# Score blocks with v and k with v in 64x64 tiles of TensorE, by token halves in two turns

## The chip, the cores and the metric

The kernel runs on one core of one Trainium2 chip. The metric is the device time of one execution in microseconds (us); before the change it is the median of three runs.

## The reference

Attention first: for each batch b (4) and head h (8) a state of 48 x 48 is carried over 768 tokens. Then a feed-forward layer with a leaky activation over all 3072 tokens.

```python
B, H, S, D = 4, 8, 768, 48
for t in range(S):
    kt, vt, rt = k[:, :, t], v[:, :, t], r[:, :, t]
    cur = einsum('bhd,bhe->bhde', u[None] * kt, vt)
    y[:, :, t] = einsum('bhd,bhde->bhe', rt, state + cur)
    state = w[None, :, :, None] * state + einsum('bhd,bhe->bhde', kt, vt)
x = y.transpose(0, 2, 1, 3).reshape(B * S, H * D)   # 3072 x 384
h = x @ w_in                                         # 384 x 2048
g = maximum(h, 0) + alpha * minimum(h, 0)
out = g @ w_out                                      # 2048 x 384
```

## The kernel before

The tokens are cut into six chunks of 128 (C = 6, L = 128). In each chunk the eight heads are worked in four pairs (q = 0 to 3); the two heads of a pair (g = 0, 1) lie on partitions 0 to 47 and 64 to 111. For a pair `attention` makes:

- the raw loads of r, k and v, and on VectorE r and k scaled by powers of w (L397);
- on TensorE the scores A = k^T r (from chunk 2 on in `triangle`, L441; in chunks 0 and 1 L450), each batch a block of 128 key tokens x 128 query tokens;
- `base`, which is the diagonal term u on the diagonal (ScalarE, L465, from the table `ident`) and the scores strictly above it (VectorE predicated copies with the mask `strict4`, L473);
- on TensorE the output y in `out`: from the state T with r (L514), then from v with `base` (L519), and, but for the last chunk, the state product of k with v (`state_product`, L528);
- y split into a high and a low half in SBUF, `x` (ScalarE L567, VectorE L571), and the state's update T (VectorE L626).

From chunk 2 on the scores are a triangle: with the key tokens in two halves of 64, the second half of the keys meets only the second half of the queries. `triangle` makes the first half's columns 128 wide and the second half's 64 wide, in 64x64 tiles, and leaves the other block out. For odd batches the key halves are swapped on the partitions, so that four tiles (row half by head, column half by key half) work side by side. The output from v and `base` still uses all 128 partitions of key tokens and all 128 query columns, in tiles of 128 rows and 64 columns; the parts of `base` in the left-out block are zeros.

The results of y go to two PSUM banks, `y[0]` (name "y", one buffer) and `y[1]` (name "hp", two buffers, which the feed-forward layer's input products use as well). Bank g holds the part of head g of the state term. The state product lies behind y in the bank "y".

From chunk 2 on `pair` puts the scores of pair q and the output and state product of pair q - 1 into one piece of work on TensorE. The first pair of a chunk has its scores alone, and the output of the last pair is a piece of its own.

The feed-forward layer runs beside it: `m_in` and `m_in_two` (L803, L756) make hp = w_in x for 128 of the 2048 columns, or for two such pieces at once with seven products in place of eight; VectorE and ScalarE make g and its halves gh and gl (L787 to L814); `m_out` (L845) adds w_out g to three banks `acc`. These are in fp32r and three products each (high with high, low with high, high with low).

The order of all instructions is written out by a planner (`Plan`): each piece has an engine, an estimated time, its reads and writes, and a rank; twelve rounds of list scheduling, forward and backward, choose the order with the earliest end. A bank that one engine reads is not read by another at the same time, so pieces of VectorE and ScalarE on one bank follow each other. Where the change gives pieces other times or other buffers, the planner makes a new order for the whole kernel.

Of the kernel before, what the change touches and what calls it, by code (L numbers as in the profile page):

```python
# [195 lines left out]
def rwkv_prelu_kernel(ctx: ExitStack, tc, rk, vkr, wP, uP, u, wall, alpha, w, r_all, k_all, v_all, oT):  # L196
# [30 lines left out]
    strict4 = fixed([128, B, L], "strict4", U8)  # L227
# [40 lines left out]
    def swapped_masks():  # L268
        add("POOL", 0.3, lambda: nc.gpsimd.memset(ones(), 1.0), w=[ones], rank=10)
        for rows, base in ((slice(0, HI), -HI), (slice(HI, 128), 0)):  # L270
            add("POOL", 0.3, lambda rows=rows, base=base: nc.gpsimd.affine_select(
                ones()[rows], ones()[rows], pattern=[[1, 128]], base=base, channel_multiplier=-1,
                compare_op=ALU.is_gt, fill=0.0), w=[ones], rank=10)
        for b in range(B):
            add("POOL", 0.3, lambda b=b: nc.gpsimd.tensor_copy(strict4()[:, b], (ones if b % 2 else strict)()),
                r=[ones, strict], w=[(strict4, b)], rank=10)
        for h in range(2):
            add("ACT", 0.5, lambda h=h: nc.scalar.activation(
                wtok()[HI * h:HI * h + HI, :, 1], wtok()[HI - HI * h:128 - HI * h, :, 0], AF.Copy), r=[(wtok, 0)],
                w=[(wtok, 1 + h)], rank=10)  # L280
# [82 lines left out]
    def attention(c, q, at):  # L363
# [3 lines left out]
        def swap(b):  # L367
            return c > 1 and b % 2 == 1

# [64 lines left out]
        A = [pb([128, B, L], f"A{g}" if not first or q % 2 == 0 else f"acc{g}") for g in range(2)]  # L434

        def triangle():

            for rows, j in ((0, 0), (0, 1), (1, 0), (1, 1)):
                for b, g in ((2 * j, 0), (2 * j + 1, 0), (2 * j, 1), (2 * j + 1, 1)):
                    o, t = (rows + b) % 2, slice(HI * rows, L)  # L440
                    nc.tensor.matmul(A[g]()[HI * o:HI * o + HI, b, t], k0()[half(g), b, HI * rows:HI * rows + HI],  # L441
                                     r()[half(g), b, t], start=(rows == 0 and j == 0), stop=(rows == 1 and j == 1),
                                     skip_group_check=True)
# [13 lines left out]
        base = [sb([128, B, L], "base", 4) for _ in range(2)]  # L457
        for g in range(2):
# [5 lines left out]
            for b in range(B):  # L464
                add("ACT", 0.39, lambda g=g, b=b: nc.scalar.activation(  # L465
                    base[g]()[:, b].rearrange("p (a t) -> p a t", a=2),
                    ident().rearrange("p (a t) -> p a t", a=2)[:, ::-1 if swap(b) else 1], AF.Copy,
                    scale=cu()[:, g, (b if c < 2 else place[b]):][:, 0:1]), r=[cu, ident], w=[(base[g], b)],
                    rank=at - 0.9 if c != 1 else -50)
        parts = [(slice(0, 128), slice(0, B), slice(HI, L)), (slice(0, HI), slice(0, B, 2), slice(0, HI)),  # L470
                 (slice(HI, 128), slice(1, B, 2), slice(0, HI))]
        for g, at_part in [(g, x) for g in range(2) for x in parts] if c > 1 else ():
            add("DVE", 0.42 if at_part is parts[0] else 0.28, lambda g=g, x=at_part: nc.vector.copy_predicated(  # L473
                base[g]()[x], strict4()[x], A[g]()[x]), r=[strict4, A[g]], w=[base[g]], rank=at - 1.5)
# [9 lines left out]
        U, plain = None, c < 2  # L484
# [4 lines left out]
        else:  # L489
            y = [pb([112, 2 * 2 * L], "y"), pb([112, 2 * L], "hp", 2)]  # L490
            U, mine = y[0], (y[0], "U")
            y_of = [(y[0], "y"), y[1]]

        def u_rows(rows):
            return U()[rows].rearrange("p (b e) -> p b e", b=B) if plain else \
                U()[rows, 2 * L:2 * L + B * D].rearrange("p (b e) -> p b e", b=B)

        def out():
            if plain:
                for b in range(B):  # L500
                    for g in range(2):
                        rows, x = (slice(0, HI) if g == 0 else half(g)), g * B + place[b]
                        nc.tensor.matmul(y()[rows, b], v().rearrange("p x e -> p (x e)")[  # L503
                            :, x * D:x * D + rows.stop - rows.start], base[g]()[:, b], start=b == 0,
                            stop=first and b == B - 1, skip_group_check=True)
                for b in () if first else range(B):
                    for g in range(2):
                        nc.tensor.matmul(y()[half(g), b], T[q]()[half(g), b], r()[half(g), b], start=False,  # L508
                                         stop=(b == B - 1), skip_group_check=True)
                return  # L510
            for j in range(2):
                for g, o in ((0, 0), (1, 1), (0, 1), (1, 0)):
                    b = j + 2 * (g ^ o)
                    nc.tensor.matmul(y[g]()[half(o), j * L:(j + 1) * L], T[q]()[half(g), b], r()[half(g), b],  # L514
                                     start=(j == 0), stop=False, skip_group_check=True)
            for j in range(2):
                for g, o in ((0, 0), (1, 1), (1, 0), (0, 1)):
                    b = j + 2 * (g ^ o)
                    nc.tensor.matmul(y[g]()[half(o), j * L:(j + 1) * L], v()[:, g * B + place[b]], base[g]()[:, b],  # L519
                                     start=False, stop=(j == 1), skip_group_check=True)  # L520
# [602 lines left out]
```

## Time and profile before

| | |
|---|---|
| device time, median of three runs | 501.57 us (501.52 to 501.6) |
| span of the profiled execution, first to last instruction | 499.7 us |
| what lies around the span (501.57 - 499.7) | 1.9 us |
| TensorE busy | 491.7 us, 98% of the span |
| VectorE, ScalarE, GpSimd busy | 373.7, 267.1, 51.4 us |
| granted clock of TensorE, mean | 0.997 of full speed |

No time of its own is listed for the profiled execution beside its span; its own time is taken as the span and the 1.9 us around it, which is the median of the runs. In the rows, PE is TensorE's matmuls, PEld its weight loads, DVE VectorE, ACT ScalarE, POOL GpSimd; L519 is line 519 of the kernel before; "y<-base,v" names the output and the inputs. A matmul of float32 operands leaves two records in the trace. Matmuls overlap, so the distance between starts says more than their durations.

### The profile page before, as it was taken

What the parts mean: (1) busy time and instruction counts of PE and PEld (TensorE: products, weight loads), DVE (VectorE), ACT (ScalarE), POOL (GpSimd) and SP (SyncE); (2) the same over time, 40 slices, a digit from 0 to 9 for tenths busy, and PEclk for the clock granted to TensorE, in tenths of its full rate; (3) what the DMA queues carried; (4) which work ended last, traced back from release to release, by engine and by line L of the source; (5) the groups of instructions that cost most, each with busy time, mean ns of one, the idle gap of its engine ahead of it and who ended that gap; (6) DMA issues with size and microseconds to landing.
All of it is one profiled execution on the core that took longest, in us unless ns stands there. A gap on an engine that the chain in (4) does not pass through costs nothing.

```text
span 499.7 us, 9759 instructions
## 1 busy us (share of the span) xinstructions
PE 491.7 (98%) x3817; PEld 405.8 (81%) x3817; DVE 373.7 (75%) x677; ACT 267.1 (53%) x612; POOL 51.4 (10%) x56
## 2 busy tenths in 40 slices
PE   8999999999999999999999999999999999999995
PEld 6877777888788887888888888888788888898984
DVE  6799999899985997768699476789475676445451
ACT  3898786786652555535455555355554443533322
POOL 4200140001020130011030020232000000000000
PEclk9999999999999999999999999999999999999998
DMA  8796765530132633313130322140230000100001
GB/s 235 240 291 193 233 202 182 190 143 1 61 124 79 184 113 96 133 35 83 56 102 30 102 68 62 54 136 16 82 72 1 0 1 1 63 1 1 2 1 68
DMA packets 24020, 46.72 MB, mean 94 GB/s; under 512 B 3488, under 2 KB 11680, under 8 KB 23968
## 3 DMA queue, kind: packets, MB, share of 16 engines
q1 hardware_dynamic: 23712, 46.03, 29.9%
q8 instruction: 32, 0.52, 0.4%
q14 instruction: 20, 0.16, 0.1%
q10 hardware_dynamic: 256, 0.00, 0.0%
HBM read 37.37 MB, written 6.29 MB: 87 GB/s over the span
## 4 chain that ended last, share of the span: by engine, by line
PE 93%; ACT 3%; DVE 1%; DMA 1%; issue 0%; ACTq 0%; DVEq 0%
PE acc L845 38%; PE hp L803 19%; PE hp L756 19%; PE A L441 3%; PE y L519 2%; PE hp L519 1%; PE y L514 1%; PE A L450 1%; PE y L503 1%; ACT base L465 1%; PE y L528 1%; PE A L845 1%; PE y L508 1%; PE acc L854 1%; PE hp L925 1%; DMA wp<-wP 1%
## 5 line engine op out<-in xcount | busy, mean ns | idle before, releaser
L803 PE MATMUL hp<-x,wh 128*128 128x512 f32 x288 | 98.1, 398 | 0.1
L845 PE MATMUL acc<-gh,wh 128*128 128x512 f32 (+1 forms) x282 | 79.9, 391 | 0.0
L845 PE MATMUL acc<-gh,wl 128*128 128x512 f32 (+1 forms) x282 | 79.6, 390 | 0.0
L845 PE MATMUL acc<-gl,wh 128*128 128x512 f32 (+1 forms) x282 | 79.5, 390 | 0.0
L787 DVE TENSOR_TENSOR g<-hp,g 128x512 f32<-128x512 f32 x48 | 32.7, 689 | 53.4 <-PE hp L756 45.0
L803 PEld LDWEIGHTS hp<-x,wh 128*128 128x128 f32 x288 | 54.0, 188 | 14.0 <-DVE g L810 0.8
L792 ACT ACTIVATE gh<-g 128x512 fp32r<-128x512 f32 x48 | 30.2, 632 | 61.2 <-DVE g L789 53.1
L756 PE MATMUL hp<-x,wh 128*128 128x256 f32 (+1 forms) x192 | 62.1, 346 | 0.0
L845 PEld LDWEIGHTS acc<-gh,wl 128*128 128x128 f32 x282 | 51.5, 188 | 11.1 <-issue 0.2
L845 PEld LDWEIGHTS acc<-gl,wh 128*128 128x128 f32 x282 | 51.2, 188 | 10.6
L465 ACT ACTIVATE base<-ident,cu 128x128 f32<-128x128 f32 x176 | 57.3, 390 | 4.3 <-DVE cu L430 3.1
L768 ACT ACTIVATE g<-hp 128x256 f32<-128x256 f32 x96 | 34.3, 381 | 46.2 <-PE hp L756 44.7
L845 PEld LDWEIGHTS acc<-gh,wh 128*128 128x128 f32 x282 | 50.7, 188 | 10.0
L803 PE MATMUL hp<-x,wl 128*128 128x512 f32 x144 | 56.8, 395 | 0.0
L810 DVE SCALAR_TENSOR_TENSOR g<-hp,alph,g 128x512 f32<-128x512 f32 x48 | 35.9, 748 | 23.0 <-ACT g L809 22.7
L424 POOL TENSOR_TENSOR rr<-rr,kk 128x384 f32<-128x384 f32 x16 | 19.4, 1212 | 275.3 <-DMA kk<-vkr 120.5
L809 ACT ACTIVATE g<-hp 128x512 f32<-128x512 f32 x48 | 28.5, 594 | 33.9 <-PE hp L803 32.8
L814 DVE TENSOR_TENSOR gl<-g,gh 128x512 fp32r<-128x512 f32 x48 | 33.7, 701 | 12.9 <-ACT gh L813 7.9
L813 ACT ACTIVATE gh<-g 128x512 fp32r<-128x512 f32 x48 | 30.2, 629 | 23.0 <-DVE g L810 21.6
L756 PEld LDWEIGHTS hp<-x,wh 128*128 128x128 f32 x192 | 36.1, 188 | 5.9 <-ACT g L768 1.4
L793 DVE TENSOR_TENSOR gl<-g,gh 128x512 fp32r<-128x512 f32 x48 | 34.6, 729 | 4.1 <-ACT gh L792 1.0
L397 DVE TENSOR_TENSOR raw<-raw,W 112x512 f32<-112x512 f32 x45 | 36.0, 810 | 0.3
(186 smaller groups left out, 851.2 us busy)
## 6 DMA issues: line engine op xcount, KB each, us to landing
wraw<-wall SPq DMA_DIRECT2D x16, 768.0 KB, 5.0
raw<-rk SPq DMA_DIRECT2D x45, 224.0 KB, 3.1
v<-vkr SPq DMA_DIRECT2D x24, 192.0 KB, 3.5
kk<-vkr SPq DMA_DIRECT2D x21, 192.0 KB, 3.1
rr<-vkr SPq DMA_DIRECT2D x16, 192.0 KB, 2.5
oT<-o SPq DMA_DIRECT2D x12, 256.0 KB, 2.3
x<-x SPq DMA_DIRECT2D x36, 64.0 KB, 2.8
oT<-g SPq DMA_DIRECT2D x5, 256.0 KB, 2.1
```

What stands on the lines that cost most here:

```text
L397: add("DVE", 0.72 if c < 2 else 0.85, lambda t=t, tab=tab: nc.vector.tensor_tensor(out=t(), in0=t(), in1=tab().broadcast_to([112, B, L]), ...
L465: add("ACT", 0.39, lambda g=g, b=b: nc.scalar.activation(base[g]()[:, b].rearrange("p (a t) -> p a t", a=2), ident().rearrange("p (a t) -> ...
L756: nc.tensor.matmul(bank()[:, cols], ws[a], xs[b], start=start and j == 0, stop=stop and j == 2, skip_group_check=True)
L768: add("ACT", 0.37, lambda: nc.scalar.activation(t()[:, cols], bank()[:, src], AF.Copy), r=[bank], w=[(t, part)], rank=rank - 100).early = 0.3
L787: add("DVE", 0.75, lambda g=g, bank=bank: nc.vector.tensor_tensor(out=g(), in0=bank(), in1=g(), op=ALU.add), r=[bank], w=[g], rank=m - 100)
L792: add("ACT", 0.64, lambda g=g, gh=gh: nc.scalar.activation(gh(), g(), AF.Copy), r=[g], w=[gh], rank=m - 100)
L793: add("DVE", 0.73, lambda g=g, gh=gh, gl=gl: nc.vector.tensor_tensor(out=gl(), in0=g(), in1=gh(), op=ALU.subtract), r=[g, gh], w=[gl], ran ...
L803: nc.tensor.matmul(hp(), a[i]()[:, k], x[c]()[:, k], start=(k == 0 and j == 0), stop=(k == NK - 1 and j == 2))
L810: add("DVE", 0.75, lambda: nc.vector.scalar_tensor_tensor(out=g(), in0=hp(), scalar=alph()[:, i:i + 1], in1=g(), op0=ALU.mult, op1=ALU.max ...
L813: add("ACT", 0.64, lambda: nc.scalar.activation(gh(), g(), AF.Copy), r=[g], w=[gh], rank=n - 100)
L814: add("DVE", 0.73, lambda: nc.vector.tensor_tensor(out=gl(), in0=g(), in1=gh(), op=ALU.subtract), r=[g, gh], w=[gl], rank=n - 99)
L845: nc.tensor.matmul(bank(), a[i]()[:, NK + k], x()[:, cols], start=(begin and j == 0), stop=(end and j == 2), skip_group_check=(c == C - 1))
```

## The change

From chunk 2 on:

- The scores' bank is laid out in blocks of 64 columns: slots 0 to 3 hold the diagonal blocks of the four batches (both key halves, one on each partition half), slots 4 and 5 the full blocks of first-half keys with second-half queries. `base` has the same layout. The diagonal term is then written into 64-column blocks from a table `eye`; per head one predicated copy takes slots 0 to 3 and one plain copy slots 4 and 5.
- The output from v and `base` is made by key halves (`out_of_tokens`), each with 64 rows and 64 columns of the array: the first key half of a batch with 128 columns, the second with 64. The zero block is left out.
- The state product is made by token halves too (`state_of_tokens`).
- Two row halves of the array write two different banks. So each of both products is done in two turns: in turn 0 row half n writes bank n, in turn 1 the other one. Turn 1 begins with an instruction on TensorE that does nothing but wait for the last matmul of turn 0 (`in_turn`).
- The joint piece of TensorE is now: state part and turn 0 of pair q - 1, scores of pair q, turn 1 of pair q - 1. For the last pair of a chunk, turn 1 follows turn 0 directly, and its state product lies in the scores' banks A0 and A1.
- The state product of the other pairs lies behind y in both banks, "y" and "hp", and the state's update is two VectorE instructions, one a bank.
- The masks on GpSimd are made for halves, and the planner gets other times for the pieces.

The core of the diff:

```diff
-        A = [pb([128, B, L], f"A{g}" if not first or q % 2 == 0 else f"acc{g}") for g in range(2)]
+        tri = c > 1
+        A = [pb([128, 8, HI] if tri else [128, B, L], f"A{g}" if not first or q % 2 == 0 else f"acc{g}")
+             for g in range(2)]
+
+        def blocks(b):
+
+            return slice(b, None, 4 + b // 2 - b)
...
                     o, t = (rows + b) % 2, slice(HI * rows, L)
-                    nc.tensor.matmul(A[g]()[HI * o:HI * o + HI, b, t], k0()[half(g), b, HI * rows:HI * rows + HI],
-                                     r()[half(g), b, t], start=(rows == 0 and j == 0), stop=(rows == 1 and j == 1),
-                                     skip_group_check=True)
+                    to = A[g]()[HI * o:HI * o + HI]
+                    nc.tensor.matmul(to[:, b] if rows else to[:, blocks(b)][:, 0:2],
+                                     k0()[half(g), b, HI * rows:HI * rows + HI],
+                                     r()[half(g), b, t], start=(rows == 0 and j == 0),
+                                     stop=(rows == 1 and j == 1), skip_group_check=True)
...
-        for g, at_part in [(g, x) for g in range(2) for x in parts] if c > 1 else ():
-            add("DVE", 0.42 if at_part is parts[0] else 0.28, lambda g=g, x=at_part: nc.vector.copy_predicated(
-                base[g]()[x], strict4()[x], A[g]()[x]), r=[strict4, A[g]], w=[base[g]], rank=at - 1.5)
+        for g in range(2) if tri else ():
+            add("DVE", 0.42, lambda g=g: nc.vector.copy_predicated(base[g]()[:, 0:B], strict4(), A[g]()[:, 0:B]),
+                r=[strict4, A[g]], w=[(base[g], b) for b in range(B)], rank=at - 1.5)
+            add("DVE", 0.28, lambda g=g: nc.vector.tensor_copy(base[g]()[:, B:B + 2], A[g]()[:, B:B + 2]),
+                r=[A[g]], w=[(base[g], B)], rank=at - 1.5)
...
-            y = [pb([112, 2 * 2 * L], "y"), pb([112, 2 * L], "hp", 2)]
-            U, mine = y[0], (y[0], "U")
-            y_of = [(y[0], "y"), y[1]]
+            y = [pb([112, 4 * L], "y"), pb([112, 4 * L], "hp", 2)]
+            U, u0, mine = y, 2 * L, [(t, "U") for t in y]
+            if alone:
+                U = mine = [pb([112, NT], f"A{g}") for g in range(2)]
+                u0 = 0
+            y_of = [(t, "y") for t in y]
...
-            for j in range(2):
-                for g, o in ((0, 0), (1, 1), (1, 0), (0, 1)):
-                    b = j + 2 * (g ^ o)
-                    nc.tensor.matmul(y[g]()[half(o), j * L:(j + 1) * L], v()[:, g * B + place[b]], base[g]()[:, b],
-                                     start=False, stop=(j == 1), skip_group_check=True)
+        def in_turn(what, turn, fn):
+
+            if turn and what in ends:
+                wait = nc.tensor.nop(nofuse=True)
+                tc.add_manual_dep(wait.ins, ends.pop(what).ins.name, mybir.DependencyInfo(
+                    mybir.DependencyClass.Sync, mybir.DependencyReason.DATA), reason="row tiles change banks")
+            ins = fn()
+            if not turn:
+                ends[what] = ins
+
+        def out_of_tokens(turn):
+
+            for late in range(2):
+                for o, n in ((0, 0), (0, 1), (1, 0), (1, 1)):
+                    g, j = n ^ turn, n ^ late
+                    b, rows = j + 2 * (g ^ o), slice(HI * n, HI * n + HI)
+                    x, t = base[g]()[rows], j * L + HI * late
+                    in_turn("y", turn, lambda: nc.tensor.matmul(
+                        y[g]()[half(o), t:(j + 1) * L], v()[rows, g * B + place[b]],
+                        x[:, b] if late else x[:, blocks(b)][:, 0:2], start=False,
+                        stop=(turn == 1 and late == 1), skip_group_check=True))
+
+        def state_of_tokens(turn):
+
+            kt = k().rearrange("p x e -> p (x e)")
+            for j in range(2):
+                for g, n in ((0, 0), (0, 1), (1, 0), (1, 1)):
+                    m, rows = n ^ turn, slice(HI * n, HI * n + HI)
+                    x, wide = g * B + place[2 * m + j], D if g else HI
+                    at_u = u0 + j * D
+                    in_turn("U" if alone else "y", turn, lambda: nc.tensor.matmul(
+                        U[m]()[HI * g:HI * g + wide, at_u:at_u + D], kt[rows, x * D:x * D + wide],
+                        v()[rows, x], start=alone and turn == 0 and j == 0,
+                        stop=(turn == 1 and j == 1), skip_group_check=True))
...
-                yield out if last else both, reads, writes, 1.5 if last else 2.0
+                def turn_of(n):
+                    out_of_tokens(n)
+                    if not last:
+                        state_of_tokens(n)
+
+                def begin():
+                    out_of_state()
+                    turn_of(0)
+
+                yield begin, lambda: turn_of(1), reads, writes, 1.0 if last else 1.3
...
+        for m in () if last or plain else range(2):
+            add("DVE", 0.3, lambda m=m: nc.vector.scalar_tensor_tensor(
+                out=T[q]()[:, 2 * m:2 * m + 2], in0=T[q]()[:, 2 * m:2 * m + 2], scalar=w128()[:, q:q + 1],
+                in1=U[m]()[:, u0:u0 + 2 * D].rearrange("p (b e) -> p b e", b=2), op0=ALU.mult, op1=ALU.add),
+                r=[mine[m], (w128, q)], w=[(T[q], m)], rank=at - 1.4)
...
         if before:
-            work.append(next(before))
...
+            begin, rest, more_reads, more_writes, more_us = next(before)
+            add_pieces([begin, scores, rest], reads + more_reads, writes + more_writes, us + more_us, at)
             finish(before)
```

## Rows read from the trace of the kernel before

**Rows 1.** The page: span; busy time and instructions of each engine.
```profile
span 499.7 us, 9759 instructions
...
PE 491.7 (98%) x3817; PEld 405.8 (81%) x3817; DVE 373.7 (75%) x677; ACT 267.1 (53%) x612; POOL 51.4 (10%) x56
```

**Rows 2.** All waits of TensorE: engine, tile, line, releaser, total us, times, longest.
```profile
PE hp L925 <- DVE unit L284: 1.2, 1, 1.2
PE A L450 <- DVE raw L397: 0.5, 1, 0.5
```

**Rows 3.** Busy time of each engine in stretches: us, then busy and instructions, clock, DMA.
```profile
80.00:140.00 60.00, 59.89 (x318) 47.56 (x320) 55.63 (x106) 43.14 (x81) 2.59 (x2) 1.00 0.33 114
140.00:280.00 140.00, 140.00 (x1175) 115.04 (x1167) 112.00 (x221) 68.21 (x171) 19.75 (x16) 1.00 0.30 89
280.00:420.00 140.00, 139.95 (x1174) 116.90 (x1173) 98.72 (x189) 67.27 (x170) 12.66 (x10) 1.00 0.18 53
```

**Rows 4.** The chain in a steady stretch: start us, us, what.
```profile
152.61 2.10 PE acc L845 x9
```

**Rows 5.** Timeline of TensorE, a joint block of chunk 2: start us, us, line, operation.
```profile
158.51 0.40 PE L845 MATMUL acc<-gl,wh 128*128 128x512 f32 x1
158.84 0.90 PE L441 MATMUL A<-raw 48*64 48x128 f32 x32
159.55 0.28 PE L514 MATMUL y<-raw,T 48*48 48x128 f32 x2
...
159.88 0.28 PE L514 MATMUL y<-raw,T 48*48 48x128 f32 x2
...
160.10 0.31 PE L519 MATMUL y<-base,v 128*48 128x128 f32 x1
...
160.25 0.27 PE L519 MATMUL y<-base,v 128*48 128x128 f32 x1
...
161.01 0.61 PE L528 MATMUL y<-v,kk 128*64 128x48 f32 x16
161.56 0.50 PE L803 MATMUL hp<-x,wh 128*128 128x512 f32 x1
161.89 0.39 PE L803 MATMUL hp<-x,wl 128*128 128x512 f32 x1
```

**Rows 6.** The same block, timeline from its first 64-column score record on.
```profile
159.32 0.41 PE L441 MATMUL A<-raw 48*64 48x64 f32 x16
```

**Rows 7.** Timeline of TensorE, the lone block of chunk 2.
```profile
176.93 0.40 PE L845 MATMUL acc<-gl,wh 128*128 128x512 f32 x1
...
179.29 0.73 PE L845 MATMUL acc<-gh,wh 128*128 128x512 f32 x2
```

**Rows 8.** Timelines, end of a chunk-5 block and the first readers of "hp".
```profile
363.64 0.27 PE L519 MATMUL y<-base,v 128*48 128x128 f32 x1
...
363.95 0.77 ACT L567 ACTIVATE x<-hp 48x256 fp32r<-48x256 f32 x2 [1.61 <-PE y L519]
...
364.75 0.86 DVE L571 TENSOR_TENSOR x<-hp,x 48x256 fp32r<-48x256 f32 x2 [0.77 <-ACT x L567]
```

**Rows 9.** VectorE's instructions by line and shape: count, busy us, mean ns.
```profile
L473 DVE COPY_PREDICATED base<-strict,A 64x128 f32<-64x128 uint8 x64 | 18.0, 298 | 0.9
...
L473 DVE COPY_PREDICATED base<-strict,A 128x256 f32<-128x256 uint8 x32 | 12.6, 440 | 0.1
...
L626 DVE SCALAR_TENSOR_TENSOR T<-T,w,y 112x192 f32<-112x192 f32 x12 | 5.0, 414 | 4.5 <-ACT x L567 4.5
```

**Rows 10.** Timelines after a joint block of chunk 3: TensorE, ScalarE, VectorE.
```profile
207.84 0.61 PE L528 MATMUL y<-v,kk 128*64 128x48 f32 x16
...
210.59 0.40 PE L756 MATMUL hp<-sxh,wraw 128*128 128x256 f32 x2
...
208.04 0.77 ACT L567 ACTIVATE x<-hp 48x256 fp32r<-48x256 f32 x2 [1.61 <-PE hp L519]
...
208.84 0.86 DVE L571 TENSOR_TENSOR x<-hp,x 48x256 fp32r<-48x256 f32 x2 [0.76 <-ACT x L567]
```

## The prediction before the run

> **What bounds the kernel now.** I read the page's engine table first: TensorE is busy in 98% of the span [rows 1]. A busy share can hide waits, so the waits of TensorE come next: they are 1.2 and 0.5 us in all [rows 2], and they lie in the first microseconds. The windows by stage say the same of the stretch that the change touches, 80 to 420 us: TensorE is busy in 59.89 of 60, 140.00 of 140 and 139.95 of 140 us at a granted clock of 1.00, the full level of 2.4 GHz, while VectorE, ScalarE and GpSimd have room in all but the first of these [rows 3]. In a steady stretch nine 512-column matmuls take 2.10 us, 0.233 each, one behind the other [rows 4]. So the time is the length of TensorE's stream; a change is worth what it adds to or takes from that stream, and work on other engines counts only where TensorE comes to wait for it.
>
> **How a block is built now.** In a joint block [rows 5] stand the scores of one pair (L441), then state part (L514), token part (L519) and state product (L528) of the pair before. Each call leaves two records, one behind the other on its tile; 16 calls of L441 are 32 records. A "round" below is one record on every tile in use. From the last 512-column matmul before the block to the second one behind it are 161.89 - 158.51 = 3.38 us; less two normal steps of 0.233 the block costs 2.91 us. Its parts:
> - Score rounds on four tiles, 128 columns wide at first, then 64. The sixteen 64-column records start at 159.32 and the state part at 159.55 [rows 6]: four rounds in 0.23, 0.058 each, or 14.4 ns a record.
> - State part, four rounds on four tiles of 128 columns: starts at 159.55, 159.66, 159.77, 159.88, 0.109 a round.
> - From the last of these rounds, which streams until 159.99, to the first token product at 160.10 nothing starts: 0.11. There the tiles change from 64 rows to 128. The first token round lasts 160.10 to 160.25, 0.15 where 0.11 is usual.
> - Token part: the second round starts at 160.25, the state product at 161.01; seven rounds of 0.109 on two tiles. With the first it is 0.91.
> - State product, eight rounds on two tiles: sixteen records in 0.61 us, whose last one lasts 0.21 by itself, so seven rounds in 0.40, 0.057 each, 0.45 in all.
> - Entry and exit: the block's first record starts 158.84 - 158.51 - 0.233 = 0.10 late, and the first two full matmuls behind it lose some 0.2 more. Both remain.
>
> **The change, part by part.**
> 1. Token part in 64x64 tiles. Eight calls become sixteen: per turn four that are 128 columns wide (two rounds) and four of 64 (two rounds). The mode is that of L441 and L514, and every row tile writes its own bank, as there, so I price the rounds by them: four of 0.109 and four of 0.058, 0.67 instead of eight of 0.109, 0.87. That is 0.20 less; the left-out zero block is the whole of it, for the halves by themselves give as many rounds as before.
> 2. The change of mode inside the block goes: 0.11, and the slow first round, 0.04. Together 0.15.
> 3. State product by token halves: twice the calls on twice the tiles, eight rounds of 48 columns as before. The tile with 64 stationary columns sets 0.058: 0.46 instead of 0.45, a loss of 0.01. From below, 48 columns at 0.109 per 128 would be 0.041 a round.
> 4. Scores: as many records of the same widths, into other columns: nothing.
> 5. The turn's wait in a joint block. Turn 1 waits for the end of turn 0. Between them stand the scores, 0.71 us (159.55 - 158.84), while a reader of a bank starts 363.95 - 363.64 = 0.31 after the last record's start [rows 8]. I take zero; behind the waiting instruction stand all of turn 1 and the next block's first matmuls. Without cover it would cost this completion, of which 0.11 is streaming, and a fresh start, 0.10 to 0.15 by the entry and the first token round above: bounds 0 and 0.35 [rows 5, 8].
>    A joint block thus gains 0.20 + 0.15 - 0.01 = 0.34, in chunk 5, where there is no state product, 0.35.
> 6. The lone block of pair 3 has no scores between the turns. In chunks 2 to 4 turn 0 of the state product stands between (four rounds, 0.23), about what a completion needs: I take 0.10 of exposed wait (bounds 0 and 0.2), so 0.24 is gained of the same 0.34; without scores it now costs 179.29 - 176.93 = 2.36 to the first full matmul behind it [rows 7]. Its second wait, for the state's bank, has turn 1 of the tokens as cover (0.33). In chunk 5 the wait is bare: 0.30, gain 0.05.
> 7. VectorE and ScalarE. Six predicated copies of 0.44 and 0.298 (2.07 us a pair) become two of 0.44 and two plain copies of 128 columns, which I put at 0.30 by the copies of as many columns: 1.48. ScalarE's eight diagonal copies go from 128 to 64 columns and can only get shorter. The state's update becomes two instructions of 0.30 to 0.41 instead of one of 0.41 [rows 9]. All this is hidden under TensorE's stream [rows 2, 3]: value zero. In 80 to 140 us, where VectorE is full, TensorE has 0.11 us without work [rows 3], and its shorter work could give that back: from 0 to 0.1.
> 8. GpSimd's masks are made once, with as many instructions to within one, and first used at 81 us: zero.
> 9. The bank "hp" is held longer, since half of the state product now lies in it too. Its readers today start during the state product: ScalarE at 208.04, VectorE done at 208.84 + 0.86 = 209.70, while the last record of the block starts at 207.84 + 0.61 - 0.21 = 208.24 and the next matmul that wants this bank starts at 210.59 [rows 10]. That is a slack of 0.89. Afterwards they start behind the last state product. A chunk-5 block shows such an order: reader 0.31 after the last record, both copies and subtractions done at 364.75 + 0.86 = 365.61, which is 1.97 after it [rows 8]; the update of the state from this bank adds 0.30 to 0.41 [rows 9]. So the bank is free 2.27 to 2.38 after the last record and wanted after 2.35: slack about zero. The order of work is planned anew and can put three more output matmuls (0.70) in front, so I take zero, with up to 0.75 (one VectorE instruction of L810's size in front) in the six blocks of chunks 2 to 4 that a two-step input product follows.
>
> **The sum.** Chunks 2 to 5 have three joint blocks and one lone block each. 9 x 0.34 + 3 x 0.35 + 3 x 0.24 + 0.05 = 3.06 + 1.05 + 0.72 + 0.05 = 4.9 us. The profiled execution's span is 499.7 [rows 1]; the runs' median is 501.57, so 1.9 us lie around the span, and I leave them. 501.57 - 4.9 = 496.7.
>
> **The rivals.**
> - *More than that* (495.0). The state product's rounds shrink to 0.041: 12 blocks x 8 x 0.017 = 1.6 us, and the 0.1 before 140 us comes back. Against it: the tile with 64 stationary columns sets 0.057 a round in L528 today, and the number of such columns stays.
> - *The gain goes into new waits* (497.7 to 501.2). Either the turn's wait shows in the joint blocks, 12 x 0.30 = 3.6 us, time 500.3; or "hp" comes late in six blocks, up to 6 x 0.75 = 4.5 us, time 501.2. For it: the slack computed above is about zero. Against it: the rest of the stream has output matmuls to put in front, and today's plan holds all waits of 340 us to a fraction of a microsecond.
> - *Short records pay by the piece* (slower). The block gets 16 short token records and, in twelve blocks, 32 state records, 12 x 48 + 4 x 16 = 640, priced here at 14.4 ns each. Today L528 starts a record every 28 ns (0.45 us for 16) and L519 one every 57 (0.91). Should the new ones go at 28 ns, however many tiles there are, they cost 640 x 13.6 = 8.7 us more, and the time is 505.4. From 14.4 + 4900/640 = 22 ns a record on, the change gains nothing. Against it stand the sixteen score records of 64 columns at 14.4 ns [rows 6], in the very mode. This is also the case in which the four tiles don't run side by side as meant.
>
> The Trainium skill has a rule of this kind: "TensorEngine Tiling (Array Packing)", section "Instruction Overhead", gives each matmul an overhead of some 60 cycles and advises against taking a tiling factor from a dimension that is already small, which 48 and 64 columns are. At 2.4 GHz this is an estimate of 25 ns a record, and the sum by it would be 640 x 10.6 = 6.8 us worse, 503.5. The trace disagrees where tiles alternate: 14.4 ns [rows 6].
>
> **How the numbers follow.** The forecast as worked out has a chance of 0.67, with a range of its own of 495.9 to 497.7 (above: the lone blocks' waits at their bounds, 0.35, and 0.05 in each joint block, 0.6; below: those waits at zero, 0.6, and some 0.01 a round of the state product in part of the blocks). More than that: 0.07. New waits: 0.20, most of it between 497.7 and 500.3. Short records by the piece: 0.06. A measurement of this kernel can tell some 0.2%, 1.0 us, from no change. Faster than 500.6: 0.67 + 0.07 + 0.14 = 0.88; within 0.2%: 0.05, all from new waits; slower: 0.07. The range for 8 in 10 takes in most of the first case above and the lower half of the second: 495.0 to 499.6.
>
> **What would show it.** Right: a joint block from last full matmul to second full one of 3.04 instead of 3.38 us, in chunk 5 0.35 below today's; no start gap between L514's rounds and the first token product; 64-column token records in rounds near 0.058; no idle time of TensorE ahead of turn 1 in joint blocks, and some 0.1 and 0.3 in lone ones; some 450 more records on TensorE, still busy 98%. Wrong: rounds of 0.11 where 64 or 48 columns are streamed; idle time before turn 1 in joint blocks; TensorE waiting for VectorE or ScalarE at the second input matmul group behind a block; a new order of the plan with waits elsewhere, above all between 80 and 140 us, where VectorE is full.

## The result and the profile after

The changed kernel takes 495.44 us (median of 4 runs, 495.07 to 496.02) beside 501.54 of the kernel before (4 runs): ratio 0.988, 95% interval 0.987 to 0.990. That is 6.1 us less, where 4.9 were forecast, and the time was put at 496.7, within 495.0 to 499.6. The profiled run took 495.62 us with a span of 493.9, so 1.7 us lie around the span; the spans differ by 499.7 - 493.9 = 5.8 us.

The page of the changed kernel, span and engine table; they answer to [rows 1]:

```profile
span 493.9 us, 10649 instructions
...
PE 486.1 (98%) x4265; PEld 403.8 (82%) x4265; DVE 368.0 (75%) x657; ACT 259.5 (53%) x612; POOL 52.9 (11%) x55
```

All waits of TensorE in it, beside [rows 2]:

```profile
PE hp L975 <- DVE unit L284: 1.2, 1, 1.2
PE A L455 <- DVE raw L394: 0.2, 1, 0.2
PE hp L542 <- PE hp L542: 0.2, 1, 0.2
```

The windows of [rows 3], of the changed kernel:

```profile
80.00:140.00 60.00, 60.00 (x287) 48.27 (x286) 56.54 (x109) 42.38 (x82) 3.56 (x2) 1.00 0.34 118
140.00:280.00 140.00, 140.00 (x1467) 115.76 (x1467) 109.00 (x210) 66.54 (x175) 21.36 (x16) 1.00 0.32 93
280.00:420.00 140.00, 139.82 (x1380) 118.16 (x1379) 100.32 (x187) 65.03 (x172) 11.98 (x10) 1.00 0.17 50
```

TensorE is still the bound, at the full clock, with 448 more records. Its stream became shorter, and nothing else became the limit.

The joint block of [rows 5], timeline of TensorE in the changed kernel. The first line is the last full matmul before the block; of each group of records on the four tiles the first stands:

```profile
157.96 0.40 PE L895 MATMUL acc<-gl,wh 128*128 128x512 f32 x1
...
158.65 0.27 PE L520 MATMUL y<-raw,T 48*48 48x128 f32 x1
...
158.76 0.27 PE L542 MATMUL y<-base,v 64*48 64x128 f32 x1
...
158.98 0.21 PE L542 MATMUL y<-base,v 64*48 64x64 f32 x1
...
159.09 0.20 PE L555 MATMUL y<-v,kk 64*64 64x48 f32 x1
...
159.27 0.90 PE L445 MATMUL A<-raw 48*64 48x128 f32 x32
159.96 0.27 PE L542 MATMUL y<-base,v 64*48 64x128 f32 x1
...
160.29 0.20 PE L555 MATMUL y<-v,kk 64*48 64x48 f32 x1
...
160.65 0.50 PE L853 MATMUL hp<-x,wh 128*128 128x512 f32 x1
160.99 0.40 PE L853 MATMUL hp<-x,wl 128*128 128x512 f32 x1
```

From full to full it is 160.99 - 157.96 = 3.03 us; 3.38 before, 3.04 forecast. The last state round starts at 158.65 and the first token round at 158.76: the gap of 0.11 is gone. The Trainium skill says in "TensorEngine Tiling (Array Packing)", section "Key Properties", that a change of tiling mode drains TensorE; the trace before agrees, with 160.10 - 159.88 = 0.22 from start to start at the change of mode, where 0.109 is usual. Two token rounds of 128 columns take 158.98 - 158.76 = 0.22, two of 64 columns 159.09 - 158.98 = 0.11. Turn 1 starts 0.69 behind the scores' first record, with no idle time ahead of it.

Over all blocks, by the same measure (last full matmul before to second full one behind, less two normal steps of 0.233), worked out from the start times of both traces:

```
block                        before   after    difference   forecast
joint, chunks 2 to 4 (9)     2.92     2.57     -0.35        -0.34
joint, chunk 5 (3)           2.47     2.12     -0.36        -0.35
lone, chunks 2 to 4 (3)      2.24     2.05     -0.18        -0.24
lone, chunk 5 (1)            1.80     1.85     +0.05        -0.05
sum of all blocks after 78 us                  -4.67        -4.9
```

The other 1.1 us of the 5.8 lie elsewhere: stalls of TensorE inside input products, which the kernel before had and the changed one hardly has (-1.38), and a start of the first full matmul at 31.19 instead of 30.92 (+0.27). A full matmul is one on all 128 rows and columns with 512 streamed columns; an input product is one of `m_in` or `m_in_two`. Each of these parts is read from one trace of either kernel. A second trace of the changed kernel (run 8) starts at 30.93 and has none of these stalls.

### The profile page after: what moved, and what is told of

The parts are those of the page before. It is cut to its first block, busy times and chain, and to the rows that moved or that the text cites. A ratio compares the mean times of both kernels' runs of the same rounds, so it can differ in the third digit from the quotient of the medians.

```text
span 493.9 us, 10649 instructions
## 1 busy us (share of the span) xinstructions
PE 486.1 (98%) x4265; PEld 403.8 (82%) x4265; DVE 368.0 (75%) x657; ACT 259.5 (53%) x612; POOL 52.9 (11%) x55
## 4 chain that ended last, share of the span: by engine, by line
PE 96%; ACT 2%; DMA 1%; DVE 0%; issue 0%; DVEq 0%; ACTq 0%
PE acc L895 39%; PE hp L853 21%; PE hp L806 20%; PE A L445 2%; PE y L520 2%; PE y L542 1%; PE A L455 1%; PE y L508 1%; PE A L895 1%; PE hp L542 1%; PE y L513 1%; PE acc L904 1%; PE hp L975 1%; DMA wp<-wP 1%; PE y L409 1%; PE A L566 0%
## 5 line engine op out<-in xcount | busy, mean ns | idle before, releaser
L421 POOL TENSOR_TENSOR rr<-rr,kk 128x384 f32<-128x384 f32 x16 | 22.6, 1413 | 273.5 <-DMA kk<-vkr 105.7
L864 DVE TENSOR_TENSOR gl<-g,gh 128x512 fp32r<-128x512 f32 x48 | 33.3, 695 | 15.0 <-ACT gh L863 8.7
L394 DVE TENSOR_TENSOR raw<-raw,W 112x512 f32<-112x512 f32 x45 | 38.1, 859 | 0.0
L470 ACT ACTIVATE base<-eye,cu 128x64 f32<-128x64 f32 x128 | 34.7, 338 | 3.8 <-DVE cu L427 3.0
L843 DVE TENSOR_TENSOR gl<-g,gh 128x512 fp32r<-128x512 f32 x48 | 32.8, 693 | 4.4 <-ACT gh L842 1.2
```

Of the source, the lines that this page charges most:

```text
L394: add("DVE", 0.72 if c < 2 else 0.85, lambda t=t, tab=tab: nc.vector.tensor_tensor(out=t(), in0=t(), in1=tab().broadcast_to([112, B, L]), ...
L470: add("ACT", 0.34 if tri else 0.39, lambda g=g, b=b: nc.scalar.activation(base[g]()[:, b], (eye if tri else ident)(), AF.Copy, scale=cu()[ ...
L843: add("DVE", 0.73, lambda g=g, gh=gh, gl=gl: nc.vector.tensor_tensor(out=gl(), in0=g(), in1=gh(), op=ALU.subtract), r=[g, gh], w=[gl], ran ...
L864: add("DVE", 0.73, lambda: nc.vector.tensor_tensor(out=gl(), in0=g(), in1=gh(), op=ALU.subtract), r=[g, gh], w=[gl], rank=n - 99)
```

## The experiments

The changed kernel is the base of each edit, unless the text says otherwise. Ratios are to the kernel before, timed beside each. That kernel's median was 501.05 to 501.54 from one such timing to another, so a difference between times that were not taken side by side holds to about 0.5 us.

**1. ScalarE's diagonal copies long again** (`e1_act128`): each writes its 64 columns twice, the second time into a spare slot.

```diff
-                    base[g]()[:, b], (eye if tri else ident)(), AF.Copy,
+                    base[g]()[:, b::6 - b][:, 0:2] if tri else base[g]()[:, b],
+                    eye()[:, None, :].broadcast_to([128, 2, HI]) if tri else ident(), AF.Copy,
```

> The changed kernel, its order of work kept, but ScalarE's diagonal copies are 128 columns long again (the second 64 go to two unused slots). Theory A, the gain beyond the blocks (some 1.4 us less waiting of TensorE in the two-step input products) comes from ScalarE's shorter diagonal copies, which stood in front of the evacuation copies: some 1.0 to 1.5 us slower than the changed kernel, 496.4 to 497.0, and the restarts of TensorE inside the input products come back. Theory B, it comes from the new order of the plan: no change, 495.2 to 495.7. Theory C, it comes from VectorE: no change here either.

498.26 us, ratio 0.995 (0.994 to 0.996): 2.8 us more than the changed kernel, above the 1.0 to 1.5 expected, while all that stands between the full matmuls from 78 us on costs the same 41.9 us. The added time lies in stalls inside input products, some 3.4 us more of them in the trace; a start earlier by 0.2 and a stretch behind the last matmul shorter by 0.6 take part of it back. ScalarE's lines in the changed kernel, and then in this one (count, busy us, mean ns, idle time before):

```profile
L470 ACT ACTIVATE base<-eye,cu 128x64 f32<-128x64 f32 x128 | 34.7, 338 | 3.8 <-DVE cu L427 3.0 <-DVE sxl L777 0.8
```

```profile
L470 ACT ACTIVATE base<-eye,cu 128x128 f32<-128x128 f32 x128 | 49.9, 398 | 6.0 <-DVE cu L427 2.8 <-DVE sxl L778 0.8
```

One place, timelines of this kernel: five copies stand in front of the copy of "hp" to "g", which ends at 231.73 + 0.38 = 232.11, and TensorE takes up the next product of this bank at 232.16, 0.46 behind the one before instead of 0.23:

```profile
229.71 1.99 ACT L470 ACTIVATE base<-eye,cu 128x128 f32<-128x128 f32 x5
...
231.73 0.38 ACT L819 ACTIVATE g<-hp 128x256 f32<-128x256 f32 x1
...
231.70 0.39 PE L807 MATMUL hp<-x,wh 128*128 128x512 f32 x1
...
232.16 0.51 PE L807 MATMUL hp<-sxh,wraw 128*128 128x256 f32 x2
```

The same place of the changed kernel; the copy to "g" is done at 231.23, half a microsecond before it is needed:

```profile
229.53 1.29 ACT L470 ACTIVATE base<-eye,cu 128x64 f32<-128x64 f32 x5
...
230.85 0.38 ACT L818 ACTIVATE g<-hp 128x256 f32<-128x256 f32 x1
...
231.52 0.39 PE L806 MATMUL hp<-x,wh 128*128 128x512 f32 x1
231.75 0.40 PE L806 MATMUL hp<-sxh,wraw 128*128 128x256 f32 x2
```

So the length of ScalarE's copies reaches TensorE. This run overstates it: a copy costs 49.9 / 128 = 0.39 us of ScalarE here, and 57.3 / 176 = 0.33 in the kernel before. It puts in 49.9 - 34.7 = 15.2 us of ScalarE's time, where the change took out some 7.

**2. VectorE's shorter work given back** (`e2_dve_more`): the plain copy also writes a second target, on half the rows.

```diff
-            add("DVE", 0.28, lambda g=g: nc.vector.tensor_copy(base[g]()[:, B:B + 2], A[g]()[:, B:B + 2]),
+            add("DVE", 0.28, lambda g=g: [nc.vector.tensor_copy(base[g]()[p, n:n + 2], A[g]()[p, B:B + 2])
+                                          for p, n in ((slice(0, 128), B), (slice(0, HI), B + 2))],
```

> The changed kernel, its order kept, with one more 64-partition copy of 128 columns per head on VectorE, so that VectorE's work for the scores is as long as before (some 0.6 us more a pair; the copy goes to unused slots). Theory C, the gain beyond the blocks comes from VectorE: 0.7 to 1.5 us slower than the changed kernel. Theories A and B: within 0.3 us of it, 495.2 to 495.8.

495.21 us, ratio 0.990 (0.988 to 0.992), span 493.5: no more than the changed kernel by the median, though one of the five runs took 497.56 and leaves the interval wide. In the trace the 32 added copies take 8.7 us of VectorE, the blocks cost 41.9 as before, and no stall comes in. VectorE's work for the scores is hidden, as step 7 had it.

**3. The kernel before with ScalarE's copies of 64 columns** (`e3_before_act64`). The diagonal term of the second half is left out, and one of VectorE's predicated copies becomes a plain one (0.41 us instead of 0.44).

```diff
-                    base[g]()[:, b].rearrange("p (a t) -> p a t", a=2),
-                    ident().rearrange("p (a t) -> p a t", a=2)[:, ::-1 if swap(b) else 1], AF.Copy,
+                    base[g]()[:, b].rearrange("p (a t) -> p a t", a=2)[:, 0:2 if c < 2 else 1],
+                    ident().rearrange("p (a t) -> p a t", a=2)[:, 0:2 if c < 2 else 1], AF.Copy,
...
-            add("DVE", 0.42 if at_part is parts[0] else 0.28, lambda g=g, x=at_part: nc.vector.copy_predicated(
+            add("DVE", 0.42 if at_part is parts[0] else 0.28, lambda g=g, x=at_part: nc.vector.tensor_copy(
+                base[g]()[x], A[g]()[x]) if x is parts[0] else nc.vector.copy_predicated(
```

> The kernel before, its order kept, with ScalarE's diagonal copies from chunk 2 on 64 columns long instead of 128; the diagonal term of the second half and the mask of one VectorE copy are left out of the computation. Theory A: the waits at ScalarE go without any change to TensorE's blocks, 1.0 to 1.4 us faster than before, 500.1 to 500.6. Theories B and C: within 0.3 us of before, 501.2 to 501.8.

500.38 us (11 runs) beside 501.05 (17): ratio 0.9988 (0.9979 to 0.9997), a gain of 0.15 to 1.05 us. In the traces the stalls inside input products shrink by 1.25 us and the span by 1.5. The direction is that of run 1; the size, at 0.6 us by the times, is about half of what the traces suggest. Part of that is which runs were traced: the one here is the fastest of the 11 (span 498.2, median 498.6), the trace before has 499.7, where the 17 runs of that kernel beside this one have 499.3 in the median.

**4. Turn 1 right behind turn 0** (`e4_bare_turn`).

```diff
-            add_pieces([begin, scores, rest], reads + more_reads, writes + more_writes, us + more_us, at)
+            add_pieces([begin, rest, scores], reads + more_reads, writes + more_writes, us + more_us, at)
```

> The changed kernel with the scores behind turn 1 instead of between the turns, so that turn 1 follows turn 0 in the joint blocks as it does in the lone ones. In the changed kernel a lone block shows 0.40 us of wait in chunk 5 and 0.15 in chunks 2 to 4, where the state's second wait is on another bank. Theory A, the scores hide all of the wait: the nine joint blocks with a state product then wait 0.3 to 0.4 us each for the end of it and the three of chunk 5 0.4 each, 12 x 0.35 to 0.40 = 4.2 to 4.8 us slower than the changed kernel, 499.7 to 500.3. Theory B, the wait costs little wherever it stands and the lone blocks are slow for another reason: under 1 us slower.

499.6 us, ratio 0.997 (0.996 to 0.999): 4.1 us more than the changed kernel. Joint blocks cost 2.96 (+0.39) and 2.51 in chunk 5 (+0.40). TensorE's waits in this kernel, and then the last record of turn 0 and the first of turn 1 in one block:

```profile
PE hp L542 <- PE hp L555: 1.6, 9, 0.2
...
PE hp L542 <- PE hp L542: 0.7, 4, 0.2
```

```profile
159.55 0.22 PE L555 MATMUL hp<-v,kk 64*64 64x48 f32 x1
159.95 0.28 PE L542 MATMUL hp<-base,v 64*48 64x128 f32 x1 [0.18 <-PE hp L555]
```

The nine and three new waits show with 0.2 each, but a block loses twice that: from start to start it is 0.40 where 0.06 is usual, and the first round behind it is 0.04 longer. The scores between the turns hide all of it.

**5. As many columns as with the zero block** (`e5_late128`): the second key half's ("late") products are 128 columns wide, with the first half's columns of `base` and into the same columns of the bank as the early ones. The second half's own diagonal block is left out.

```diff
-                    x, t = base[g]()[rows], j * L + HI * late
+                    x, t = base[g]()[rows], j * L
...
-                        x[:, b] if late else x[:, blocks(b)][:, 0:2], start=False,
+                        x[:, blocks(b)][:, 0:2], start=False,
```

> The changed kernel in which the second key half's products with v run over 128 columns like the first half's (the full block is added a second time in place of the second half's own diagonal block; the computation is changed in that). It gives back the left-out zero block alone. Theory A, the round prices hold (0.109 for 128 columns, 0.055 for 64): four rounds a block become 0.054 longer, 16 x 4 x 0.054 = 3.5 us slower than the changed kernel, 498.7 to 499.2. Theory B, records cost by the piece: no change.

498.17 us, ratio 0.994 (0.992 to 0.995), span 496.1. Each of the 16 blocks costs 0.208 more, 3.3 in all; the time rises by 2.7 over the changed kernel, less than the 3.5 expected. In the trace the start is 0.2 earlier, the stretch behind the last matmul 0.5 shorter, and a stall of 0.25 of the changed kernel's trace is absent.

**6. State product with 128 rows again** (`e6_state128`), behind the tokens of turn 1. The new function `state_of_all`, not shown, makes it in one go with half as many calls:

```diff
-                    if not last:
-                        state_of_tokens(n)
+                    if not last and n:
+                        state_of_all()
```

> The changed kernel with the state product in tiles of 128 rows behind turn 1, in one go, as half as many calls. Theory A, making the state product by halves is worth nothing by itself and pays by sparing the change of tile mode: a block gets back the gap of 0.11 and the slow first round of 0.04, 12 x 0.15 = 1.8 us, and the lone blocks of chunks 2 to 4 lose the cover of their wait, some 0.2 each: 2.0 to 2.6 us slower than the changed kernel. Theory B, twice the calls cost as much as the mode change: within 0.5 us of it.

497.49 us, ratio 0.993 (0.991 to 0.995). The blocks cost 2.41 more in sum: 0.14 in each joint block, 0.39 in each lone one of chunks 2 to 4. The 0.14 is what the prediction put at 0.15 for the change of mode, less 0.01 for the state's rounds; in the lone block the turn's wait is bare besides. So a state product by halves is itself no faster than one over all rows; it pays by sparing the change of mode and by covering the turn's wait of the lone blocks.

**7. The lone blocks joined with the next chunk's first scores** (`e7_joined`).

```diff
-        U, plain, alone = None, c < 2, q == P - 1
+        U, plain, alone = None, c < 2, last and q == P - 1
...
-        if q < P - 1:
+        if q < P - 1 or c < C - 1:
...
+            if q == 0 and c > 2:
+                at = jobs[-1][0] + 1
```

> The changed kernel with the lone block of the last pair of chunks 2, 3 and 4 joined with the scores of the first pair of the next chunk, which are made some four steps earlier; its state product then lies behind y. Theory A: blocks of 1.03 and 2.05 us become one of 2.57, 3 x 0.51 = 1.5 us faster than the changed kernel, 493.6 to 494.1. Rival: the buffers that the next chunk's first pair holds for longer (base, v, k) bring waits or another order: no change or up to 1 us slower.

497.13 us, ratio 0.992 (0.991 to 0.993). The blocks gain 1.58 us, but three new stalls come in behind the joined blocks, in start-to-start steps 1.43, 0.47 and 0.87 us. TensorE's waits in this kernel:

```profile
PE hp L806 <- DVE g L837: 1.8, 2, 1.2
...
PE hp L806 <- ACT g L818: 0.2, 1, 0.2
```

The longest of them, timelines of TensorE and VectorE: the instruction that clears bank "hp" starts on VectorE only at 259.54, behind two others.

```profile
258.60 0.68 DVE L394 TENSOR_TENSOR raw<-raw,W 112x512 f32<-112x512 f32 x1
258.71 0.39 PE L806 MATMUL hp<-x,wh 128*128 128x512 f32 x1
259.20 0.41 DVE L771 TENSOR_TENSOR o<-o 128x256 f32<-128x256 f32 x1
259.54 1.27 DVE L837 TENSOR_TENSOR g<-hp,g 128x512 f32<-128x512 f32 x2
...
260.27 0.39 PE L806 MATMUL hp<-x,wh 128*128 128x256 f32 x1 [1.17 <-DVE g L837]
```

**8. The changed kernel once more** (`e8_changed_again`), without an edit.

> The changed kernel once more, beside the next two, so that they are compared on the same chip: 495.0 to 495.7.

495.47 us, ratio 0.989 (0.988 to 0.991), span 493.4, blocks again 41.9, and no stall of 0.1 us or more inside the input products from 78 us on.

**9 and 10. The joined kernel with its blocks begun earlier, or set closer** (`e9_joined_early`, `e10_joined_dense`).

```diff
-        space, before = SPACE.get(c, (3.5, 16.0))
+        space, before = SPACE.get(c, (3.5, 18.0))    # run 9
+        space, before = SPACE.get(c, (3.0, 16.0))    # run 10
```

> The joined kernel with the pairs of chunks 3 to 5 begun 18 instead of 16 steps ahead of their chunk. In the joined kernel the blocks are 1.6 us shorter, as expected, but TensorE waits 1.3, 0.4 and 0.8 us at the first two-step input products of chunks 3 and 4, where VectorE has the token sums, the state updates and the next pair's work at the same time. Theory A, it is this crowding that costs: two steps earlier the waits go and the time is 493.5 to 494.3. Theory B, the buffers held longer cost by themselves: it stays at 496.5 or more.

> The joined kernel with the pairs of a chunk 3.0 instead of 3.5 steps apart, so that the joined block lies two steps earlier while the first pair begins as before. Theory A (crowding at the token sums): 493.5 to 494.5. Theory B (buffers): 496.5 or more.

497.40 us (0.991 to 0.994) and 497.44 us (0.992 to 0.995). The longest stall, 1.4 and 2.0 us, moves with the block from 258.7 to 250.5. So what VectorE has to do at the old place in the chunk isn't its cause. Both times fit the expectations' theory B, that the buffers held longer cost by themselves, but neither run shows this mechanism.

**11 and 12. Another time told to the planner for VectorE's scaling (L394)**, in the joined kernel (`e11_joined_est`) and in the changed one (`e12_changed_est`).

```diff
-            add("DVE", 0.72 if c < 2 else 0.85, lambda t=t, tab=tab: nc.vector.tensor_tensor(
+            add("DVE", 0.72 if c < 2 else 1.3, lambda t=t, tab=tab: nc.vector.tensor_tensor(
```

> The joined kernel in which the planner is told 1.3 instead of 0.85 us for VectorE's scaling of r and k from chunk 2 on. In the traces this instruction takes 0.68 us by itself and up to 1.5 while GpSimd works on the next pair's products, and in the joined kernel such a stretch of VectorE lies in front of the sums that free the input products' banks. Theory A, TensorE's waits in the joined kernel come from this order of VectorE's work: the planner now puts the sums first, the waits of 2.6 us go for the most part, 494.0 to 495.0. Theory B, VectorE is simply too full after the joined block: no better than 496.5.

> The changed kernel with the same estimate (1.3 instead of 0.85 us). TensorE has hardly any wait left to win there: within 0.5 us of the changed kernel, 495.0 to 495.9, or slower by a worse order.

498.67 us (0.994 to 0.996) and 497.89 us (0.992 to 0.994): both slower. The stall on "g" stays in run 11 at 1.6 us, and in run 12 the order alone, with the instructions unchanged, costs 2.4 us. TensorE's waits of run 12 show 1.0 us of it, and its first block of chunk 2 stands 0.85 us later, at 81.93 instead of 81.08; the rest isn't placed, for the run traced, at 497.22, is 0.7 faster than the median.

```profile
...
PE acc L895 <- ACT gh L842: 1.0, 1, 1.0
```

What exactly makes VectorE late behind a joined block stays open, and no version beat the changed kernel.

## Why the prediction was right, point by point

- **Steps 1 to 5, the joint blocks: right.** 0.35 and 0.36 against 0.34 and 0.35. Step 1's zero block is worth 0.208 in run 5 (0.20), steps 2 and 3 together 0.14 in run 6 (0.14). Step 5's turn wait costs nothing under the scores; bare, it costs 0.39 to 0.40 (run 4), somewhat above the upper bound of 0.35.
- **Step 3, right in sum.** In the joint block above, the state's records on a tile with 64 stationary columns start at 159.19 and 159.25, 58 ns apart, and on one with 48 at 159.18 and 159.23, 45 ns apart; the wider tile binds, as assumed. The rival *more than that* rested on rounds below this and falls with them; only its 0.1 us before 140 us came back (60.00 of 60 us busy, 59.89 before), and in start-to-start steps that place was worth 0.38, as step 7 below has it.
- **Step 6, lone blocks: mis-sized.** In the lone block of chunk 2 turn 1 starts 0.40 behind the last token record of turn 0, with the state product's 0.23 between them; in chunk 5 it is 0.40 as well, bare:

```profile
176.07 0.21 PE L542 MATMUL hp<-base,v 64*48 64x64 f32 x1
176.11 0.40 PE L555 MATMUL A<-v,kk 64*64 64x48 f32 x16
176.47 0.28 PE L542 MATMUL hp<-base,v 64*48 64x128 f32 x1
...
400.79 0.21 PE L542 MATMUL hp<-base,v 64*48 64x64 f32 x1
...
401.19 0.28 PE L542 MATMUL hp<-base,v 64*48 64x128 f32 x1 [0.18 <-PE hp L542]
```

  The prediction put the exposed part at 0.10 and 0.30; by the costs of the blocks it is 0.16 and 0.40, 0.06 and 0.10 more. For the four blocks that is 3 x 0.06 + 0.10 = 0.28 of the 4.9, and the lone block of chunk 5 became 0.05 slower.
- **Step 7, valued at nothing: wrong for ScalarE, right for VectorE's work on the scores.** The traces show 1.38 us of stalls inside input products gone. In the kernel before there are seven such places of 0.11 to 0.38, 1.63 us in all; one of 0.25 is left after, and run 8 has none. In five of the seven, 1.14 us in sum, four diagonal copies stand right in front of ScalarE's copy of "hp" to "g", and TensorE goes on when that copy ends. Run 1 shows that the length of the diagonal copies reaches TensorE, run 3 that with shorter ones 0.10 of these 1.14 is left, run 2 that VectorE's work on the scores doesn't count. How much of the 6.1 us this is stays between 0.15, the lower end of run 3's interval, and 1.1 us. The step failed by its reading: [rows 2, 3] show no wait there. In one such place of the kernel before, TensorE streamed three matmuls of 0.117, started the next at 233.27 instead of 233.17 and lost another 0.11 behind it; ScalarE's copy ended at 232.83 + 0.39 = 233.22:

```profile
231.54 1.27 ACT L465 ACTIVATE base<-ident,cu 128x128 f32<-128x128 f32 x4
...
232.82 0.52 PE L756 MATMUL hp<-x,wraw 128*128 128x256 f32 x3
232.83 0.39 ACT L768 ACTIVATE g<-hp 128x256 f32<-128x256 f32 x1
...
233.27 0.51 PE L756 MATMUL hp<-sxh,wraw 128*128 128x256 f32 x2
...
233.61 0.28 PE L756 MATMUL hp<-sxl,wraw 128*128 128x256 f32 x1
```

  Five steps of 0.117 are 0.585; from 232.82 to 233.61 it is 0.79. The records overlap, so TensorE's waits and busy time show it as busy. The waits of its weight loads (PEld), which [rows 2] leave out, do name the releaser, here in the kernel before and then in run 1. They don't tell the loss: the changed kernel has 15 such waits, 3.4 us, and hardly a stall.

```profile
PEld hp L756 <- ACT g L768: 2.6, 12, 0.3
```

```profile
PEld hp L807 <- ACT g L819: 8.8, 26, 0.6
```

  The other two of the seven places are not shown to be the diagonal copies' doing. The largest, 0.38 at 136.37, ends with VectorE's L810, as this weight load of the kernel before shows; run 3 keeps 0.27 of it, and run 2 doesn't bring it back. At 265.75, 0.11, ScalarE's copy to "g" had itself waited 0.29 for VectorE; the same product has the 0.25 that is left in the changed kernel's trace, and none in run 8. What the change did to these two, by the new order of the plan or otherwise, stays open.

```profile
136.87 0.19 PEld L803 LDWEIGHTS hp<-x,wh 128*128 128x128 f32 x1 [0.54 <-DVE g L810]
```

- **Step 9, bank "hp": right, and close.** After the joint block of chunk 3 that answers to [rows 10], last state record, copies and subtractions of the changed kernel:

```profile
206.44 0.22 PE L555 MATMUL y<-v,kk 64*64 64x48 f32 x1
...
206.71 0.77 ACT L615 ACTIVATE x<-hp 48x256 fp32r<-48x256 f32 x2 [1.73 <-PE y L555]
...
207.51 0.31 DVE L678 SCALAR_TENSOR_TENSOR T<-T,w,hp 112x96 f32<-112x96 f32 x1 [0.41 <-ACT x L615]
207.84 0.86 DVE L619 TENSOR_TENSOR x<-hp,x 48x256 fp32r<-48x256 f32 x2
...
208.81 0.40 PE L806 MATMUL hp<-sxh,wraw 128*128 128x256 f32 x2
```

  The bank is free at 208.70, 2.26 after the last record (2.27 to 2.38 forecast), and wanted at 208.81: no wait, with 0.11 to spare. The rival *new waits* was thus close here; in run 7 waits of TensorE for VectorE on this bank, behind the joined blocks, ate the whole gain of the blocks.
- **Short records by the piece: wrong.** Two rounds, which are eight 64-column token records, take 0.11 us, 14 ns a record, as the scores do [rows 6].
- **The sum.** Of 5.8 us of span, 4.67 are the blocks, by the steps of the prediction; the remainder is the stalls of step 7 less a later start. The forecast was 1.3 us too high: 0.9 by the span, that is 1.1 by this remainder less 0.2 that the blocks gave short, then 0.2 by what lies around the span (1.7 instead of 1.9), and 0.2 because the run traced took longer than the median. The time lies inside the range of 495.0 to 499.6, but below 495.9, where the range of the forecast as worked out ends. Only the share kept for the rival *more than that* (495.0) takes it in, and that rival's shorter rounds didn't come. So the blocks were right by their mechanism, and that the time fell inside the range was in part luck.

## What to carry to other kernels

Price a block in TensorE's stream by rounds, one record on each tile in use; with records as short as the 48 columns here, the widest stationary operand sets the round. And keep neighbours in one tiling mode, with other work between two turns on a bank. Where TensorE's stream is the bound, look for stalls of 0.1 to 0.4 us in its start-to-start steps, since neither its waits nor its busy share show them; the waits of its weight loads tell whom to suspect. An edit that shortens another engine's work in front of a reader of TensorE's banks is then not free of effect, and a new order of a planned schedule can by itself cost 2 us.

## What the runs showed of the hardware

- TensorE's wait for its own last matmul costs 0.40 us from start to start when nothing stands between (400.79 to 401.19 in the changed kernel, 159.55 to 159.95 in run 4).
- Tiles run on independently: behind the state product of turn 0 in the joint block above, the two 48-column tiles begin their scores at 159.27 and 159.28, 45 ns after their last state record, and the two 64-column ones at 159.31 and 159.33, 58 ns after theirs. So the lag goes into the next records without a gap.
- VectorE's scaling (L394, two operands from SBUF) takes 0.68 us alone and up to 1.5 us while GpSimd multiplies, as here in the changed kernel, beside GpSimd's instruction from 287.42 to 289.36. Every slower one overlaps GpSimd. In one place the long one is GpSimd's: two scalings inside its product that starts at 180.39 take 0.68 each, and the product 3.15 where the same line takes 1.0 at 209.25.

```profile
286.85 1.05 DVE L394 TENSOR_TENSOR raw<-raw,W 112x512 f32<-112x512 f32 x1
...
288.42 1.50 DVE L394 TENSOR_TENSOR raw<-raw,W 112x512 f32<-112x512 f32 x1
```

  The Trainium skill, "SBUF — State Buffer", section "Who interferes with whom", says that a VectorE instruction with two inputs from SBUF contends with a GpSimd instruction that reads SBUF; the trace agrees, with the 1.5 against 0.68 us above.
